# Turning key sums in one product group, a shorter warm-up and chunked weight multiplication in an attention and FFN kernel

## The chip, the cores and the metric

The kernel runs on one core of one Trainium2 chip. The metric is the device time of one execution in microseconds (us). A median of several executions is given for each kernel; some seven in ten executions lie within 0.3 us of it, single ones up to 1 us away. A ratio between two kernels is the mean time of one kernel's fast runs over that of the other's of the same rounds, so it is not quite the ratio of the medians. A profile is one execution; its span starts at the first instruction and is some 1.7 us shorter than the device time.

The engines are TensorE (PE in the profile; PEld is its weight load), VectorE (DVE), ScalarE (ACT), GpSimd (POOL) and SyncE (SP), which issues the loads.

## The reference

A polynomial sketch attention (4 batches, 4 heads, 1088 positions, head size 32) feeds a SwiGLU block of 128 to 1536 to 128:

```python
def phi(x):
    a = np.einsum('rd,bhsd->bhsr', S1, x)
    b = np.einsum('rd,bhsd->bhsr', S2, x)
    return np.einsum('bhsi,bhsj->bhsij', a, b).reshape(*x.shape[:-1], r * r)   # r = 8
q_p, k_p = (phi(q), phi(k))
kv = np.einsum('bhsf,bhsd->bhfd', k_p, v)
z = np.sum(k_p, axis=2)
num = np.einsum('bhsf,bhfd->bhsd', q_p, kv)
den = np.einsum('bhsf,bhf->bhs', q_p, z)[..., None] + 1e-06
x = (num / den)          # to (4352, 128)
g = x @ w_gate
out = (g * (1 / (1 + np.exp(-g))) * (x @ w_val)) @ w_out
```

The inputs come as 64-bit floats. The kernel narrows the weights itself: VectorE and ScalarE split exponent and mantissa, GpSimd multiplies the two parts.

## The kernel before

Batch 0 is computed first, with nothing beside it but the narrowing of weights; batches 1 to 3 are computed in pieces among the FFN products of the batch before. For each batch `key_values` sums k_p times v over the positions, and z, the sum of k_p, is added and turned so that the features stand on the partitions. Two steps did this for z: a group that adds (the result has 32 rows per head), and a turning by the identity, the same as for kv. In batches 1 to 3:

```python
        zs = feature_sums(phk)            # GpSimd: partial sums of k_p, 128 x 256
        ...
        key_values(kvp[:, 0, :], phk, 0, NC)
        for h in range(H):
            nc.tensor.matmul(
                kvp[32 * h : 32 * h + 32, 1, 0:F], ones[:], zs[:, h, :], start=True, stop=True
            )
        kvs = apool.tile([P, 2, F], FP32, tag="kvs", name="kvs")
        nc.scalar.copy(kvs[:], kvp[:, :, 0:F])
        ...
        for t in range(2):
            turn_kv(kvs[:, t, :], kzp[:, t, :])      # products with the identity, 2 halves each
        nc.scalar.copy(kvz[:], kzp)
```

Batch 0 does the same with `sel` in place of `ones`, and with VectorE copying between the steps (`zs0`, then `kvs0`). Its last third of `key_values` comes behind the adding group. Ahead of everything stand products of constants that nobody reads (`keep_warm`), which keep TensorE busy until the inputs arrive. The sketch (S1 and S2 turned into `s12`) comes behind them; then VectorE transposes k:

```python
    keep_warm(98, 32)
    keep_warm(18, 64)
    ...
    for h in range(H):                    # the sketch
        nc.tensor.matmul(srep[32 * h : 32 * h + 32, 0 : 2 * R], s32[:], ident[...], ...)
    keep_warm(3, ps=bank("acc"))          # 3 products of 512 columns
    ...                                   # s12 on VectorE
    for c in fpieces:
        turn_k(*c)
```

The loads are issued in the order S1, k, part of q, weight pieces 0 of gate and value, v (four parts), the rest.

Of the kernel before, what the change touches and what calls it, by code (L numbers as in the profile page):

```python
# [7 lines left out]
FP32 = mybir.dt.float32  # L8
# [4 lines left out]
ALU = mybir.AluOpType  # L13
# [4 lines left out]
def kernel(  # L18
# [28 lines left out]
    nc = tc.nc  # L47
    P = nc.NUM_PARTITIONS
    B, H, S, Dh = q.shape
# [6 lines left out]
    F = R * R  # L56
# [18 lines left out]
    apool = ctx.enter_context(tc.tile_pool(name="attn", bufs=1))  # L75
# [7 lines left out]
    def bank(tag=None):  # L83
        if tag is None:
            tag = free_banks[turn[0] % len(free_banks)]
            turn[0] += 1
        return psum.tile([P, TB], FP32, tag=tag, name="bank")

    def wide(tag):
        return psum.tile([P, 2, TB], FP32, tag=tag, name=tag)  # L90
# [8 lines left out]
    wg = const.tile([P, NCH, P], FP32, name="wg")  # L99
# [30 lines left out]
    weights = dict(wg=(wg, moe_w_gate), wv=(wv, moe_w_val), wo=(wo, moe_w_out))  # L130
# [36 lines left out]
    ident = const.tile([P, P], FP32, name="ident")  # L167
    ones = const.tile([P, Dh], FP32, name="ones")
    own = const.tile([P, H], FP32, name="own")
    sel = const.tile([P, Dh], FP32, name="sel")  # L170
# [17 lines left out]
    def keep_warm(n, w=TB, ps=None):  # L188


        if ps is None:
            ps = bank(free_banks[turn[0] % len(free_banks)])
        for _ in range(n):
            nc.tensor.matmul(  # L194
                ps[0:32, 0:w], warm[:, 0:32], warm[:, 0:w], start=True, stop=True
            )

    def narrow(dst, raw, shape):






        words = raw.bitcast(I32)
        pat = "p (n w) -> p n w" if len(shape) == 2 else "p c (n w) -> p c n w"
        words = words.rearrange(pat, w=2)
        lo = words[..., 0].bitcast(U32)
        hi = words[..., 1]
        first = len(shape) == 2  # L210
        tag = "s" if first else ""
        e, m = (
            stage.tile(shape, I32, tag=n + tag, name=n, bufs=6) for n in ("exp", "man")
        )
        f = m[:].bitcast(FP32)
        nc.vector.tensor_scalar(e[:], hi, 0x7FF00000, None, op0=ALU.bitwise_and)  # L216
        nc.vector.tensor_scalar(
            m[:], hi, 0xFFFFF, 0x100000, op0=ALU.bitwise_and, op1=ALU.bitwise_or
        )
        yield  # L220
        nc.scalar.activation(e[:], e[:], AF.Relu, bias=rebias[: shape[0], :], scale=8.0)  # L221
        nc.scalar.activation(f, m[:], AF.Copy, scale=2.0**-20)  # L222
        yield
        nc.vector.scalar_tensor_tensor(  # L224
            out=e[:], in0=hi, scalar=-(1 << 31), in1=e[:],
            op0=ALU.bitwise_and, op1=ALU.bitwise_or,
        )
        nc.vector.scalar_tensor_tensor(  # L228
            out=f, in0=lo, scalar=2.0**-52, in1=f, op0=ALU.mult, op1=ALU.add
        )  # L230
        mul = nc.vector if first else nc.gpsimd
        mul.tensor_tensor(out=dst, in0=f, in1=e[:].bitcast(FP32), op=ALU.mult)  # L232
        if not first:
            load_next()
        yield
# [26 lines left out]
    def turn_q(x0, n):  # L262
        nc.vector.transpose(
            out=qT[:, x0 : x0 + n, :, :].rearrange("p x a t -> p (x a) t"),
            in_=qld[:, 2 * x0 : 2 * x0 + 2 * n, :],
        )
# [54 lines left out]
                stop=(c + 4 >= NC),  # L321
            )

    def turn_kv(kvs, kzp):

        for half in range(2):
            nc.tensor.matmul(  # L327
                kzp[F * half : F * half + F, 0:P], kvs, ident[:], start=True, stop=True
            )

    def query_products(x0, n, tags):

# [108 lines left out]
    def feature_sums(phk):  # L441

        rows = phk[:].rearrange("p c h i j -> p c (h i j)")
        s = apool.tile([P, 4, H * F], FP32, tag="zs", name="zs")
        add = lambda o, a, b: nc.gpsimd.tensor_tensor(out=o, in0=a, in1=b, op=ALU.add)  # L445
        add(s[:], rows[:, 0:4, :], rows[:, 4:8, :])
        add(s[:, 0:2, :], s[:, 0:2, :], s[:, 2:4, :])
        add(s[:, 0, :], s[:, 0, :], s[:, 1, :])
        add(s[:, 0, :], s[:, 0, :], rows[:, 8, :])
        return s[:, 0, :].rearrange("p (h f) -> p h f", h=H)  # L450

    def attention(b):

        for c0, c1 in kpieces:
            turn_k(c0, c1)
            if c1 == NC and b + 1 < B:
                load_k(b + 1)
            yield
        phk = apool.tile([P, NC, H, R, R], FP32, tag="phk", name="phk")
        prods = [key_products(wide(t)[:, 0, :], *c) for t, c in zip("ab", kpieces)]  # L460
        key_features(phk, prods[0], *kpieces[0])
        yield
        key_features(phk, prods[1], *kpieces[1])
        zs = feature_sums(phk)
        yield
        kvp = wide("a")
        key_values(kvp[:, 0, :], phk, 0, NC)
        for h in range(H):
            nc.tensor.matmul(
                kvp[32 * h : 32 * h + 32, 1, 0:F], ones[:], zs[:, h, :], start=True, stop=True  # L470
            )
        kvs = apool.tile([P, 2, F], FP32, tag="kvs", name="kvs")
        nc.scalar.copy(kvs[:], kvp[:, :, 0:F])
        if b + 1 < B:
            load_v(b + 1, [nc.sync] * 4)
        turn_q(*steps[0])
        yield
        kvz = apool.tile([P, 2, P], FP32, tag="kvz", name="kvz", bufs=2)
        kzp = wide("b")[:, 0, 0 : 2 * P].rearrange("p (t n) -> p t n", t=2)
        for t in range(2):  # L480
            turn_kv(kvs[:, t, :], kzp[:, t, :])
        nc.scalar.copy(kvz[:], kzp)
        kvz = kvz[:, 0, :], kvz[:, 1, :]
        yield
        tags = "ab"
        for i, (x0, n) in enumerate(steps):
            phq = query_features(n, query_products(x0, n, tags))
            if i + 1 < len(steps):
                turn_q(*steps[i + 1])
            elif b + 1 < B:  # L490
                load_q(b + 1)
            yield
            divide(b, x0, n, totals(n, phq, kvz, side_by_side(tags[0])))
            tags = tags[::-1]
            yield
# [5 lines left out]
    acc = {}  # L501
# [4 lines left out]
    def unit(i, j, late=False):  # L506

        t0, n = blocks[i]
        g, u = bank(), bank()
        for o, w in ((g, wg), (u, wv)):  # L510
            nc.tensor.matmul(  # L511
                o[:, 0:n], w[:, j, :], xT[:, t0 : t0 + n], start=True, stop=True
            )
        sg = fpool.tile(
            [P, BW], FP32, tag="sgl" if late else "sg", name="sg", bufs=6 if late else 3
        )
        nc.scalar.activation(sg[:, 0:n], g[:, 0:n], AF.Silu)  # L517
        hj = fpool.tile([P, BW], FP32, tag="h", name="hj", bufs=27)
        hidden[i, j] = hj
        todo.append((i, j))  # L520
        if late:
            nc.scalar.copy(hj[:, 0:n], u[:, 0:n])
            lates.append((hj[:, 0:n], sg[:, 0:n]))
        else:
            nc.vector.tensor_tensor(  # L525
                out=hj[:, 0:n], in0=sg[:, 0:n], in1=u[:, 0:n], op=ALU.mult
            )
# [38 lines left out]


    keep_warm(98, 32)
    keep_warm(18, 64)
    fills = {(w, i): narrow_w(w, i) for w in weights for i in range(len(pieces[w]))}  # L570

    def part(name, i):

        next(fills[name, i], None)
# [6 lines left out]
    for h in range(H):  # L581
# [4 lines left out]
            start=True,  # L586
            stop=True,
        )
    keep_warm(3, ps=bank("acc"))
    sTv = srep[:, 0 : 2 * R].rearrange("p (t r) -> p t r", t=2)  # L590
    nc.vector.tensor_tensor(
        out=s12[:],
# [24 lines left out]
    part("wg", 0)  # L617
    part("wv", 0)
    zq = apool.tile([P, H * F], FP32, tag="zq", name="zq")
    kvs, zs = (apool.tile([P, F], FP32, name=x) for x in ("kvs0", "zs0"))  # L620
    kvz = [apool.tile([P, P], FP32, name=x) for x in ("kvz0", "kvz1")]
    qbs.append(query_copy(n, *pss[1]))
    nc.scalar.copy(zq[:], kz)
    part("wg", 0)
    key_values(kv, phk, *fpieces[0])
    key_values(kv, phk, *fpieces[1])
    phq = query_features(n, pss, qbs)
    zp = bank("g2")
    for h in range(H):
        nc.tensor.matmul(  # L630
            zp[32 * h : 32 * h + 32, 0:F], sel[:], zq[:, F * h : F * h + F],
            start=True, stop=True,
        )
    key_values(kv, phk, *fpieces[2])
    nc.vector.tensor_copy(zs[:], zp[:, 0:F])
    turn_q(*steps[1])
    for t, s, to, tag in ((1, zs, None, "g0"), (0, kvs, kv, "g1")):
        if to is not None:
            nc.vector.tensor_copy(s[:], to)
        ps = bank(tag)  # L640
        turn_kv(s[:], ps)
        nc.scalar.copy(kvz[t][:], ps[:, 0:P])
    part("wv", 0)
    part("wg", 0)
    nd = totals(n, phq, kvz, ([bank(t) for t in ("g2", "acc")], side_by_side("a")[0]))
# [19 lines left out]
    part("wg", 2)  # L665
    part("wv", 2)
    turn_q(*steps[2])
    unit(0, 2, late=True)
    part("wg", 2)
    unit(1, 0, late=True)  # L670
    pss = query_products(*steps[2], "ab")
    qbs = [query_copy(steps[2][1], *ps) for ps in pss]
# [98 lines left out]
```

## Time and profile before

| | before |
|---|---|
| device time, median | 323.42 us (323.35 to 323.60, 3 runs) |
| span of the profile | 321.5 us |
| TensorE busy | 312.6 us, 97% |
| first FFN product | 16.06 us |
| FFN product that waits for weight piece 1 | 19.69 us |

The timeline of TensorE in batch 0 (start and busy time in us, engine, line, operation, form, count):

```profile
10.36 0.88 PE L304 MATMUL b<-phk,vld 128*32 128x64 f32 x48
11.05 0.31 PE L630 MATMUL bank<-zq,sel 128*32 128x64 f32 x8
11.18 0.51 PE L304 MATMUL b<-phk,vld 128*32 128x64 f32 x24
```

L304 is the product with v, L630 the group that adds the key sums: it stands for only 0.13 us between two parts of L304. And GpSimd's multiplication of the second pieces (L232), in its timeline:

```profile
18.46 1.18 POOL L232 TENSOR_TENSOR wg<-man,exp 128x256 f32<-128x256 f32 x1 [2.54 <-DVE man L228]
19.60 0.75 POOL L232 TENSOR_TENSOR wv<-man,exp 128x256 f32<-128x256 f32 x1
```

The second is the same work as the first and took 0.43 us less.

### The profile page before, as it was taken

The numbers are of one execution on the slowest core, as the hardware profiler recorded it, in microseconds if no ns is written. First come the engines' busy times: TensorE is split into PE (matmuls) and PEld (weight loads), VectorE is DVE, ScalarE is ACT, GpSimd is POOL, SyncE is SP. The second block draws the span as 40 slices with busy tenths as digits, with TensorE's granted clock in tenths as the row PEclk, the third lists the DMA queues.
The fourth block names the chain that finished last, engine by engine and source line by source line (L and its number), as shares of the span: only waits on it lengthen the run. The fifth ranks groups of instructions, "written<-read, shape, count | busy, mean of one in ns | idle before, by whom it ended". The sixth has DMA issues, their size and how long they took to land.

```text
span 321.5 us, 5554 instructions
## 1 busy us (share of the span) xinstructions
PE 312.6 (97%) x2276; PEld 189.9 (59%) x2276; DVE 156.7 (49%) x330; ACT 99.0 (31%) x227; POOL 37.6 (12%) x53
## 2 busy tenths in 40 slices
PE   8889999999999999999999999999999999999994
PEld 6545555656556665555666656555667655556672
DVE  4887888653466522544643543354544332322331
ACT  3467555322121222322322322323222222222220
POOL 2322333173000140000000060000000000000000
PEclk9999999999999999999999999999999999999998
DMA  7543580204041201100210100000010100100101
GB/s 203 156 150 100 157 248 0 71 0 96 1 96 22 69 17 55 27 0 2 31 65 0 22 2 0 14 12 2 0 27 0 20 0 2 26 0 0 24 2 20
DMA packets 25017, 13.99 MB, mean 44 GB/s; under 512 B 18848, under 2 KB 23072, under 8 KB 24992
## 3 DMA queue, kind: packets, MB, share of 16 engines
q1 hardware_dynamic: 24304, 13.56, 16.5%
q8 instruction: 18, 0.29, 0.4%
q10 hardware_dynamic: 688, 0.08, 0.2%
q14 instruction: 7, 0.06, 0.1%
HBM read 11.41 MB, written 2.23 MB: 42 GB/s over the span
## 4 chain that ended last, share of the span: by engine, by line
PE 89%; DVE 5%; ACT 2%; issue 1%; DMA 1%; POOL 0%; DVEq 0%
PE bank L511 50%; PE bank L539 28%; PE a L348 2%; PE a L398 2%; PE b L348 1%; PE bank L194 1%; PE a L304 1%; ACT exp L221 1%; DVE exp L216 1%; DMA raw<-in_moe_w_out_dram 1%; PE b L398 1%; PE a L273 1%; PE b L327 1%; PE bank L316 1%; ACT man L222 0%
## 5 line engine op out<-in xcount | busy, mean ns | idle before, releaser
L525 DVE TENSOR_TENSOR hj<-sg,bank 128x384 f32<-128x384 f32 (+1 forms) x138 | 72.7, 529 | 122.6 <-PE bank L511 117.8
L517 ACT ACTIVATE sg<-bank 128x384 f32<-128x384 f32 (+1 forms) x144 | 67.8, 473 | 167.1 <-PE bank L511 165.5
L511 PE MATMUL bank<-xT,wg 128*128 128x384 f32 (+1 forms) x288 | 114.1, 478 | 2.3 <-POOL wg L232 1.1
L511 PE MATMUL bank<-xT,wv 128*128 128x384 f32 (+1 forms) x288 | 111.9, 470 | 0.3 <-DVE hj L525 0.3
L539 PE MATMUL bank<-hj,wo 128*128 128x384 f32 (+1 forms) x288 | 109.1, 471 | 0.1
L511 PEld LDWEIGHTS bank<-xT,wv 128*128 128x128 f32 x288 | 54.0, 190 | 35.2 <-DVE hj L525 3.6
L511 PEld LDWEIGHTS bank<-xT,wg 128*128 128x128 f32 x288 | 52.5, 190 | 36.8 <-issue 3.9
L539 PEld LDWEIGHTS bank<-hj,wo 128*128 128x128 f32 x288 | 54.0, 190 | 33.0 <-issue 2.4
L445 POOL TENSOR_TENSOR zs<-phk 128x1024 f32<-128x1024 f32 x3 | 7.1, 2352 | 107.1 <-PE bank L511 106.0
L376 DVE TENSOR_TENSOR phq<-a,qb 128x384 f32<-128x384 f32 (+1 forms) x11 | 5.8, 531 | 10.7 <-ACT qb L362 10.7
L362 ACT COPY qb<-a 128x384 f32<-128x384 f32 (+1 forms) x11 | 5.1, 462 | 15.0 <-PE b L348 8.6
L348 PE MATMUL b<-qT,sq 32*64 32x192 f32 (+1 forms) x176 | 9.2, 324 | 0.0
L348 PE MATMUL a<-qT,sq 32*64 32x192 f32 (+1 forms) x176 | 9.2, 324 | 0.0
L221 ACT ACTIVATE exp<-exp,rebias 128x384 int32<-128x384 int32 (+3 forms) x15 | 8.3, 550 | 2.8 <-DVE exp L216 2.0
L419 DVE STREAM_TRANSPOSE dT<-a 128x384 f32<-128x384 f32 (+1 forms) x8 | 4.4, 550 | 7.8 <-PE a L398 7.8
L362 ACT COPY qb<-b 128x384 f32<-128x384 f32 (+1 forms) x11 | 5.1, 464 | 9.7 <-PE b L348 6.4
L224 DVE SCALAR_TENSOR_TENSOR exp<-raw,exp 128x384 int32<-128x384 int32 (+2 forms) x14 | 7.4, 532 | 0.9 <-ACT exp L221 0.9
L348 PEld LDWEIGHTS a<-qT,sq 32*64 32x64 f32 x176 | 5.5, 131 | 3.9 <-issue 3.0
L376 DVE TENSOR_TENSOR phq<-b,qb 128x384 f32<-128x384 f32 (+1 forms) x11 | 5.8, 527 | 4.2 <-ACT qb L362 4.2
L555 DVE STREAM_TRANSPOSE o<-bank 128x384 f32<-128x384 f32 (+1 forms) x12 | 6.7, 561 | 2.2 <-PE bank L539 1.8
L232 POOL TENSOR_TENSOR wg<-man,exp 128x384 f32<-128x384 f32 (+2 forms) x5 | 4.6, 928 | 21.1 <-DVE man L228 21.1
L228 DVE SCALAR_TENSOR_TENSOR man<-raw,man 128x384 f32<-128x384 uint32 (+2 forms) x14 | 6.9, 493 | 0.0
(93 smaller groups left out, 164.4 us busy)
## 6 DMA issues: line engine op xcount, KB each, us to landing
kld<-in_k_dram SPq DMA_DIRECT2D x4, 544.0 KB, 4.7
vld<-in_v_dram SPq DMA_DIRECT2D x12, 144.0 KB, 4.0
qld<-in_q_dram SPq DMA_DIRECT2D x3, 544.0 KB, 3.8
raw<-in_moe_w_out_dram SPq DMA_DIRECT2D x4, 384.0 KB, 3.2
out_dram<-o SPq DMA_DIRECT2D x32, 48.0 KB, 1.8
raw<-in_moe_w_gate_dram SPq DMA_DIRECT2D x3, 384.0 KB, 3.2
raw<-in_moe_w_val_dram SPq DMA_DIRECT2D x3, 384.0 KB, 3.4
out_dram<-o SPq DMA_DIRECT2D x14, 40.0 KB, 1.7
```

What stands on the lines that cost most here:

```text
L221: nc.scalar.activation(e[:], e[:], AF.Relu, bias=rebias[: shape[0], :], scale=8.0)
L224: nc.vector.scalar_tensor_tensor(out=e[:], in0=hi, scalar=-(1 << 31), in1=e[:], op0=ALU.bitwise_and, op1=ALU.bitwise_or,)
L228: nc.vector.scalar_tensor_tensor(out=f, in0=lo, scalar=2.0**-52, in1=f, op0=ALU.mult, op1=ALU.add)
L348: nc.tensor.matmul(parts[g][F * half : F * half + F, t, 0:w], sq[r, t, :, :].rearrange("p i j -> p (i j)"), qT[r, x0 : x0 + n, half, :], s ...
L362: nc.scalar.copy(qb[:, :, 0:w], both[:, :, 1, 0:w])
L376: nc.vector.tensor_tensor(out=phq[:, 2 * pr : 2 * pr + 2, 0:w], in0=both[:, :, 0, 0:w], in1=qb[:, :, 0:w], op=ALU.mult,)
L398: nc.tensor.matmul(halves(nd[t])[half][32 * h : 32 * h + 32, 0:w], kvz[t][r, 32 * h : 32 * h + 32], phq[r, h, 0:w], start=True, stop=True,)
L445: add = lambda o, a, b: nc.gpsimd.tensor_tensor(out=o, in0=a, in1=b, op=ALU.add)
L511: nc.tensor.matmul(o[:, 0:n], w[:, j, :], xT[:, t0 : t0 + n], start=True, stop=True)
L517: nc.scalar.activation(sg[:, 0:n], g[:, 0:n], AF.Silu)
L525: nc.vector.tensor_tensor(out=hj[:, 0:n], in0=sg[:, 0:n], in1=u[:, 0:n], op=ALU.mult)
L539: nc.tensor.matmul(acc[i][:, 0:n], wo[:, j, :], hidden.pop((i, j))[:, 0:n], start=(j == 0), stop=(j == NCH - 1),)
```

## The change

The intent: one group both turns and adds the key sums, so that a copy and half of the turning fall away; fewer unread products, so that the sketch comes sooner; the second weight pieces multiplied by chunk of 128 columns, so that the first chunk can be used sooner; and one step of the third piece issued ahead of a unit. The core of the diff:

```diff
-        mul.tensor_tensor(out=dst, in0=f, in1=e[:].bitcast(FP32), op=ALU.mult)
+        p2 = e[:].bitcast(FP32)
+        cuts = [slice(0, 1), slice(1, 2)] if shape[1] == 2 else [slice(None)]
+        for c in cuts:
+            mul.tensor_tensor(out=dst[:, c], in0=f[:, c], in1=p2[:, c], op=ALU.mult)
...
+    def turn_sums(sums, weights, ps):
+        for h in range(H):
+            for half in range(2):
+                nc.tensor.matmul(
+                    ps[F * half : F * half + F, Dh * h : Dh * h + Dh],
+                    sums[:, F * h : F * h + F],
+                    weights,
+                    start=True, stop=True,
+                )
...     # batches 1 to 3
-        for h in range(H):
-            nc.tensor.matmul(
-                kvp[32 * h : 32 * h + 32, 1, 0:F], ones[:], zs[:, h, :], start=True, stop=True
-            )
-        kvs = apool.tile([P, 2, F], FP32, tag="kvs", name="kvs")
-        nc.scalar.copy(kvs[:], kvp[:, :, 0:F])
+        turn_sums(zs, ones[:], kvp[:, 1, :])
+        kvs = apool.tile([P, F], FP32, tag="kvs", name="kvs")
+        kvz = [apool.tile([P, P], FP32, tag="kvz%d" % t, name="kvz", bufs=2) for t in range(2)]
+        nc.scalar.copy(kvs[:], kvp[:, 0, 0:F])
+        nc.scalar.copy(kvz[1][:], kvp[:, 1, 0:P])
...
-    keep_warm(18, 64)
+    keep_warm(9, 64)
...
-    keep_warm(3, ps=bank("acc"))
+    keep_warm(2, ps=bank("acc"))
+    keep_warm(16, 32, ps=bank("acc"))
...     # batch 0
-    for h in range(H):
-        nc.tensor.matmul(
-            zp[32 * h : 32 * h + 32, 0:F], sel[:], zq[:, F * h : F * h + F], ...
-        )
+    ps = bank("g2")
+    turn_sums(zq, sel[:], ps)
+    nc.scalar.copy(kvz[1][:], ps[:, 0:P])
     key_values(kv, phk, *fpieces[2])
-    nc.vector.tensor_copy(zs[:], zp[:, 0:F])
     turn_q(*steps[1])
...
-    unit(0, 2, late=True)
     part("wg", 2)
+    unit(0, 2, late=True)
```

More of the change, by code (lines that the diff above doesn't have):

```diff
@@ L322, in unit_sums, with turn_kv @@
             )
-    def turn_kv(kvs, kzp):
+    def turn_kv(kvs, ps):
         for half in range(2):
             nc.tensor.matmul(
-                kzp[F * half : F * half + F, 0:P], kvs, ident[:], start=True, stop=True
+                ps[F * half : F * half + F, 0:P], kvs, ident[:], start=True, stop=True
             )
+    def turn_sums(sums, weights, ps):
[5 more added lines that the diff above has]
+                    weights,
+                    start=True,
+                    stop=True,
+                )
     def query_products(x0, n, tags):
@@ L449, in feature_sums @@
         add(s[:, 0, :], s[:, 0, :], rows[:, 8, :])
-        return s[:, 0, :].rearrange("p (h f) -> p h f", h=H)
+        return s[:, 0, :]
     def attention(b):
@@ L477, in attention @@
         yield
-        kvz = apool.tile([P, 2, P], FP32, tag="kvz", name="kvz", bufs=2)
-        kzp = wide("b")[:, 0, 0 : 2 * P].rearrange("p (t n) -> p t n", t=2)
-        for t in range(2):
-            turn_kv(kvs[:, t, :], kzp[:, t, :])
-        nc.scalar.copy(kvz[:], kzp)
-        kvz = kvz[:, 0, :], kvz[:, 1, :]
+        ps = wide("b")[:, 0, :]
+        turn_kv(kvs[:], ps)
+        nc.scalar.copy(kvz[0][:], ps[:, 0:P])
         yield
@@ L619 @@
     zq = apool.tile([P, H * F], FP32, tag="zq", name="zq")
-    kvs, zs = (apool.tile([P, F], FP32, name=x) for x in ("kvs0", "zs0"))
-    kvz = [apool.tile([P, P], FP32, name=x) for x in ("kvz0", "kvz1")]
+    kvs = apool.tile([P, F], FP32, tag="kvs", name="kvs")
+    kvz = [apool.tile([P, P], FP32, tag="kvz%d" % t, name="kvz", bufs=2) for t in range(2)]
     qbs.append(query_copy(n, *pss[1]))
@@ L627 @@
     phq = query_features(n, pss, qbs)
-    zp = bank("g2")
-    for h in range(H):
-        nc.tensor.matmul(
-            zp[32 * h : 32 * h + 32, 0:F], sel[:], zq[:, F * h : F * h + F],
-            start=True, stop=True,
-        )
+    ps = bank("g2")
+    turn_sums(zq, sel[:], ps)
+    nc.scalar.copy(kvz[1][:], ps[:, 0:P])
     key_values(kv, phk, *fpieces[2])
-    nc.vector.tensor_copy(zs[:], zp[:, 0:F])
     turn_q(*steps[1])
-    for t, s, to, tag in ((1, zs, None, "g0"), (0, kvs, kv, "g1")):
-        if to is not None:
-            nc.vector.tensor_copy(s[:], to)
-        ps = bank(tag)
-        turn_kv(s[:], ps)
-        nc.scalar.copy(kvz[t][:], ps[:, 0:P])
+    nc.vector.tensor_copy(kvs[:], kv)
+    ps = bank("g1")
+    turn_kv(kvs[:], ps)
+    nc.scalar.copy(kvz[0][:], ps[:, 0:P])
     part("wv", 0)
@@ L667 @@
     turn_q(*steps[2])
+    part("wg", 2)
     unit(0, 2, late=True)
-    part("wg", 2)
     unit(1, 0, late=True)
```

## The prediction

> **What bounds the kernel now.** I read the page's busy shares and chain first, then the chain of its first 20 us, then the timelines of the groups that the change touches. The page says that the span is TensorE work:
>
> ```profile
> PE 312.6 (97%) x2276; PEld 189.9 (59%) x2276; DVE 156.7 (49%) x330; ACT 99.0 (31%) x227; POOL 37.6 (12%) x53
> ...
> PE 89%; DVE 5%; ACT 2%; issue 1%; DMA 1%; POOL 0%; DVEq 0%
> ```
>
> Busy shares of a pipelined engine say little, so I checked the starts of the products: behind 20 us a 128x384 product starts every 0.323 us (two per matrix product), with extra gaps of more than 0.2 us only five times, all between 32 and 78 us. A product that is added or removed after about 80 us is therefore paid in full. Before 20 us another regime holds. The chain there (start, us, what) is:
>
> ```profile
> 4.90 0.34 PE bank L582 x8
> ...
> 5.33 0.23 DVE s L591
> 5.55 1.41 DVE kT L257 x3
> ...
> 12.14 0.12 DVE kvs L639
> ...
> 12.31 0.44 PE bank L327 x4
> ...
> 13.34 0.59 DVE dT L419
> ...
> 18.05 0.34 DVE man L228
> ...
> 18.46 1.19 POOL wg L232
> ...
> 19.69 4.20 PE bank L511 x12
> ```
>
> Here VectorE carries the work, and two hops hand over: the sketch (L582, S1 and S2 turned) before the key transposes, and GpSimd's multiplication of the second weight piece (L232) before the FFN unit. The view of waits gives that hop its price on TensorE:
>
> ```profile
> PE bank L511 <- POOL wg L232: 1.1, 1, 1.1
> ```
>
> From 19.69 us on TensorE runs almost without a gap to 28 us, and what follows hangs on it, so time won at 19.69 us should reach the end.
>
> For the product groups I used timelines of TensorE around 182, 194 and 200 us, in the steady part (batch 3; start, busy, line, form, count):
>
> ```profile
> 182.09 0.80 PE L273 MATMUL a<-s,kT 128*64 128x64 f32 x20
> 182.72 0.64 PE L273 MATMUL b<-s,kT 128*64 128x64 f32 x16
> 183.29 0.91 PE L511 MATMUL bank<-xT,wg 128*128 128x384 f32 x2
> ...
> 193.16 1.21 PE L304 MATMUL a<-phk,vld 128*32 128x64 f32 x72
> 194.19 0.29 PE L469 MATMUL a<-zs,ones 128*32 128x64 f32 x8
> 194.42 0.91 PE L511 MATMUL bank<-xT,wg 128*128 128x384 f32 x2
> ...
> 200.42 0.66 PE L327 MATMUL b<-ident,kvs 128*64 128x128 f32 x8
> 201.01 0.59 PE L511 MATMUL bank<-xT,wg 128*128 128x384 f32 x1
> ```
>
> The starts are what to read: 72 of L304 go in 1.03 us (14 ns each, four column groups side by side), 36 of L273 in 1.20 us (33 ns with the way out; 29 ns start to start, as two every 58.5 ns), the 8 of L469 cost 0.23 us and the 8 of L327 0.59 us (55 ns start to start, plus 0.20 us on the way out).
>
> **What the Trainium skill says.** "TensorEngine Tiling (Array Packing)", Overview, Key Properties: a change of tiling mode drains TensorE. The trace agrees: a 384-column product followed by one of another shape (128*32, 128*64, 64*32) takes 0.415 us to the next start, not 0.323, so 0.09 us per change. "TensorE: Matmul & The Clock Gate", LDWEIGHTS: a weight load costs its columns over 1.2 GHz, so 64 columns would be 53 ns, by the page. The trace gives 58.5 ns per pair of halves for L273 (64 weight columns, 64 moving) but 56 ns per four for L304 (32 weight columns, also 64 moving): I read the difference as the 64-column load being the limit in L273. "SBUF — State Buffer", Terms and "SBUF: two separate sides": VectorE instructions with two SBUF inputs and GpSimd exclude each other for whole instructions. The trace agrees: the same 128x256 multiplication on GpSimd took 1.18 us at 18.46 us, under two such VectorE instructions that end at 19.06 us, and 0.75 us at 19.60 us.
>
> **The change part by part.**
>
> *Turned sums.* Before, each batch added the key sums in 8 instructions (4 products of 64 columns, 32-column weights) and turned them in 4 of the 8 instructions of L327. After, 16 instructions (4 heads, 2 halves, two passes) have the sums as 64-column weights and only 32 moving columns. Streaming 32 columns would allow about 14 ns each (half of 27 ns, two halves at once), but the weight load should hold them at L273's pitch of 29 ns. In batches 1 to 3: before 0.23 + 0.59 = 0.82 us. After: mode change behind L304 0.09 us, 16 x 29 ns = 0.46 us, way out 0.12 us, together 0.67 us; L327 with 4 instructions fewer is 0.59 - 4 x 0.055 = 0.37 us; sum 1.04 us. That is +0.22 us per batch and, all three lying in the steady part, +0.67 us. ScalarE's copies become three (about 0.19, 0.27 and 0.27 us) in place of 0.27 and 0.37 us; it is 31% busy, which costs nothing.
>
> *The same in batch 0.* VectorE loses a copy of 0.23 us (L635) and TensorE the first L327, but that copy is not what the end waits for: kvs comes at 12.07 us behind the transposition of q, while its products were done at 11.69 us. After the change the 16 products stand ahead of the last 24 of L304: instead of 0.13 us they take 0.09 + 0.46 + 0.12 = 0.67 us. The last L304 ends at about 12.25 us rather than 11.69, and kvs starts at about 12.30 rather than 12.07: +0.2 us on the chain.
>
> *Unread products.* Nine products of 64 columns at 53 ns are 0.48 us less before the sketch, which moves from 4.90 to about 4.4 us. But the transposes behind it need k: that load is issued at 1.26 us and lands 4.0 us later, at 5.28 us. They start at 5.47 us now and can start at 5.35 at best: -0.1 us. The 16 short products in place of one of 512 only keep the array busy for as long.
>
> *Multiplication by chunk.* The unit needs only the first 128 columns of the piece. A 128x128 multiplication took 0.46 us elsewhere; with the 0.43 us that it is shut out, the first half ends near 19.35 us rather than 19.65. wv follows at 19.35 + 2 x 0.42 = 20.2 us, so its product can start at about 20.24 us instead of 20.44. Gain about 0.25 us.
>
> *Order.* ScalarE converts the third piece before the third unit; ScalarE and VectorE both have idle time there (VectorE idles 0.95 us at 23.67), and TensorE does not wait on either between 20.5 and 28 us. 0.
>
> Sum: +0.67 + 0.2 - 0.1 - 0.25 = +0.5 us, so 323.9.
>
> **The rivals.** First: the weight load is not the limit, and the 16 products go at 14 ns. Then a batch costs 0.09 + 0.22 + 0.12 + 0.37 = 0.80 us, as before, and batch 0 loses nothing; -0.35 us in all, 323.1. For it speaks that the pitch of 29 ns rests on one group; against it, that L273 and L304 differ only in the weight columns and the column groups that follow from them. I give it 0.3. Second: k does not gate (or lands earlier) and the full 0.48 us of the shorter warm-up comes through: 0.35 us better than the sum. Against it stands the landing time. Third: the shorter warm-up lets the array get its full clock later; the first products ran at half pace (53 ns for 64 bf16 columns at 4 us, 220 ns for 512 at 5.5 us), so a later switch could cost up to 1 us. Against it: the stretch up to the transposes is filled as before. Fourth: a piece multiplied earlier starts the next weight loads earlier and upsets the DMA order; the loads are released by VectorE's reading of the raw piece, not by GpSimd, so I expect nothing.
>
> **Range and chances.** 0.7 x 323.9 + 0.3 x 323.1 is about 323.7. The repeats of before lie within 0.25 us. The lower end takes the first and second rivals together, 322.7; the upper end takes a slower pitch (40 ns: 16 x 11 ns x 3 = 0.5 us more) or a little of the third, 324.5. Two per cent is 6.5 us, and no part is larger than 1 us: within 2% is all but certain.
>
> **What would show it.** The new group's starts per instruction: 29 ns (sum right) or 14 (first rival), and the time from the last L304 product of batch 3 to the next FFN product: 0.7 us against 0.26. The first transposition of k at 5.35 us. kvs in batch 0 at 12.2 (12.3 less 0.1). First use of the second wg piece at 19.5 us. From there to 170 us the distance between the same FFN products of the two traces should grow by 0.22 us at each batch; if it grows elsewhere, or if the full clock comes later, the prediction is wrong.

## The result

The changed kernel took 324.70 us (median of 4 runs, 324.49 to 324.88) against 323.51 (323.35 to 323.78, 4 runs): ratio 1.0036, 95% interval 1.0018 to 1.0053. It is slower by 1.2 us, which is within 2%, and it lies 0.2 us above the upper end of the range on record. The direction was right, the size was not.

The page's busy shares and the chain by engine:

```profile
PE 313.4 (97%) x2298; PEld 190.6 (59%) x2298; DVE 156.6 (48%) x329; ACT 98.9 (31%) x230; POOL 37.8 (12%) x55
...
PE 88%; DVE 5%; DMA 2%; ACT 2%; issue 1%; POOL 0%; SPq 0%; DVEq 0%
```

TensorE has 0.8 us more busy time, and the chain now contains a load (DMA 2%, was 1%). The chain of the first 20 us says which:

```profile
1.26 4.19 DMA kld<-in_k_dram
...
5.47 1.50 DVE kT L260 x3
...
10.97 0.88 PE b L307 x48
11.85 0.59 PE bank L338 x16
12.44 0.52 PE b L307 x24
...
12.98 0.24 DVE kvs L645
...
14.29 0.59 DVE dT L434
...
19.42 0.91 POOL wg L235
...
20.37 4.32 PE bank L522 x12
```

The transposes of k start at 5.47 us, as in before, though the sketch is done 0.48 us earlier: they wait for k. L307 (the product with v, L304 before) starts at 10.97 in place of 10.36 us, and L338, the new group, takes 0.59 us between the two parts of L307 where the old one took 0.13. The view of waits names both loads:

```profile
PEld b L307 <- DMA vld<-in_v_dram: 0.8, 1, 0.8
...
DVE kT L260 <- DMA kld<-in_k_dram: 0.5, 1, 0.5
```

The timeline of TensorE in batch 3, against the same stretch in the prediction:

```profile
194.47 1.21 PE L307 MATMUL a<-phk,vld 128*32 128x64 f32 x72
195.61 0.66 PE L338 MATMUL a<-ones,zs 128*64 128x32 f32 x16
196.20 0.91 PE L522 MATMUL bank<-xT,wg 128*128 128x384 f32 x2
...
202.20 0.44 PE L330 MATMUL b<-ident,kvs 128*64 128x128 f32 x4
202.57 0.91 PE L522 MATMUL bank<-xT,wg 128*128 128x384 f32 x2
```

From L307's start to the next FFN product it is 1.73 us, was 1.26; the turning of kv is 0.37 us, was 0.59. GpSimd's timeline for the second pieces (the line is now L235):

```profile
19.42 1.31 POOL L235 TENSOR_TENSOR wg<-man,exp 128x128 f32<-128x128 f32 x2 [2.55 <-DVE man L228]
20.70 0.86 POOL L235 TENSOR_TENSOR wv<-man,exp 128x128 f32<-128x128 f32 x2
```

**Where the time came from.** Both kernels have the same 864 FFN product instructions in the same order, so I took the distance between the starts of the same one in the two traces, and list where it changes:

| start in before, us | distance, us | step | what lies there |
|---|---|---|---|
| 16.06 | +0.953 | +0.953 | batch 0 |
| 19.69 | +0.679 | -0.274 | first chunk of wg |
| 20.44 to 20.83 | +0.794 | +0.115 | wv, second chunks |
| 74.79 | +1.264 | +0.470 | batch 1, turned sums |
| 79.34 | +1.045 | -0.219 | batch 1, turning of kv |
| 118.97 | +1.522 | +0.477 | batch 2, turned sums |
| 125.56 | +1.304 | -0.218 | batch 2, turning of kv |
| 194.42 | +1.780 | +0.476 | batch 3, turned sums |
| 201.01 | +1.562 | -0.219 | batch 3, turning of kv |

Everywhere else it stays constant within 0.03 us. Batches 1 to 3 thus cost 0.251 + 0.259 + 0.257 = 0.77 us, and the chunks gave 0.16 us. The first row, 0.953 us, needs the experiments: part of it is v's late landing in this one execution. The full clock came early in this profile (its record begins at 4.27 us), so a late clock has no part in it.

### The profile page after: what moved, and what is told of

Its sections match the earlier page's. It is cut to its first block, busy times and chain, and to the rows that moved or that the text cites. A ratio compares the mean times of both kernels' runs of the same rounds, so it can differ in the third digit from the quotient of the medians.

```text
span 323.0 us, 5603 instructions
## 1 busy us (share of the span) xinstructions
PE 313.4 (97%) x2298; PEld 190.6 (59%) x2298; DVE 156.6 (48%) x329; ACT 98.9 (31%) x230; POOL 37.8 (12%) x55
## 4 chain that ended last, share of the span: by engine, by line
PE 88%; DVE 5%; DMA 2%; ACT 2%; issue 1%; POOL 0%; SPq 0%; DVEq 0%
PE bank L522 50%; PE bank L550 28%; PE a L363 2%; PE a L413 2%; DMA kld<-in_k_dram 1%; PE b L363 1%; PE a L307 1%; ACT exp L221 1%; DVE exp L216 1%; DMA raw<-in_moe_w_out_dram 1%; PE b L413 1%; PE a L276 1%; PE a L338 1%; PE bank L319 1%; ACT man L222 0%
## 5 line engine op out<-in xcount | busy, mean ns | idle before, releaser
L235 POOL TENSOR_TENSOR wg<-man,exp 128x128 f32<-128x128 f32 (+1 forms) x6 | 4.8, 802 | 20.7 <-DVE man L228 20.7
```

## The experiments

Theory A: the product groups cost the time, in all four batches. Theory B: v's late landing is brought about by the change and is the main cost. Later I called V the theory that the loads gate the start-up and scatter from execution to execution, and W that the shorter warm-up lets TensorE's full clock come late in some executions. All runs gave correct results. "Start" in the tables is the distance from the profile of before at its FFN product of 16.06 us, and "rest" is how much the distance has changed by 201.01 us; both are read from one execution, as above. The profile of before that they are measured from is of a fast execution (323.16 us).

### One part at a time

**e1_steady**: before, with the turned sums in batches 1 to 3 alone (the change's diff above, that part; other tags).

```diff
-        for h in range(H):
-            nc.tensor.matmul(
-                kvp[32 * h : 32 * h + 32, 1, 0:F], ones[:], zs[:, h, :], start=True, stop=True
-            )
+        turn_sums(zs, ones[:], kvp[:, 1, :])
...
+        nc.scalar.copy(kvs[:], kvp[:, 0, 0:F])
+        nc.scalar.copy(kvz[1][:], kvp[:, 1, 0:P])
```

> Before plus one part: the turned sums in batches 1 to 3 alone (16 products of 32 moving columns in place of 8 + 4). Theory A (the product groups cost the time): each of the three batches adds 0.25 us of TensorE work that nothing hides, as the two traces show at 74.8, 119.0 and 194.4 us, so +0.75 us, about 324.2 us; the group should take about 0.59 us from its first product to the next group. Theory B (the late landing of v in batch 0 is what costs, and the groups only move work about): 0 to +0.3 us. The start up to 20 us should be as before in both.

**e2_batch0**: before, with the turned sums in batch 0 alone.

```diff
-            zp[32 * h : 32 * h + 32, 0:F], sel[:], zq[:, F * h : F * h + F],
...
+    turn_sums(zq, sel[:], ps)
+    nc.scalar.copy(kvz[1][:], ps[:, 0:P])
     key_values(kv, phk, *fpieces[2])
-    nc.vector.tensor_copy(zs[:], zp[:, 0:F])
```

> Before plus one part: the turned sums in batch 0 alone. Theory A: kvs starts 0.3 us later than in before when v lands as early as there, because 16 products with a mode change on each side stand ahead of the last 24 products with v; +0.3 us at the end, about 323.8 us. Theory B: v is not touched by this part, so the first product with v still starts at 10.4 us; if it starts near 10.9 us here too, then the shift of v is not due to the warm-up.

**e3_warm**: before, with the shorter warm-up alone.

```diff
-    keep_warm(18, 64)
+    keep_warm(9, 64)
...
-    keep_warm(3, ps=bank("acc"))
+    keep_warm(2, ps=bank("acc"))
+    keep_warm(16, 32, ps=bank("acc"))
```

> Before plus one part: the shorter warm-up (9 products fewer, 16 short ones in place of one long). Theory A: the sketch comes 0.48 us earlier, the first transposition of k waits for its load as before, and the time stays within 0.1 us of before. Theory B (the warm-up shifts the fetches or the loads so that v lands late): the first product with v starts near 10.9 us in place of 10.4, +0.3 to +0.6 us. The forecast on record had -0.1 us.

**e4_chunk**: before, with the chunks alone.

```diff
-        mul.tensor_tensor(out=dst, in0=f, in1=e[:].bitcast(FP32), op=ALU.mult)
+        cuts = [slice(0, 1), slice(1, 2)] if shape[1] == 2 else [slice(None)]
+        for c in cuts:
+            mul.tensor_tensor(out=dst[:, c], in0=f[:, c], in1=p2[:, c], op=ALU.mult)
```

> Before plus one part: the second weight pieces multiplied by chunk on GpSimd. The product that waits for them starts 0.25 to 0.3 us earlier (at 19.4 in place of 19.69 us), the gain is carried to the end less about 0.1 us that the second operand takes back: -0.15 to -0.25 us, about 323.2 us. A rival: the two GpSimd instructions more are shut out by VectorE once more each, and the gain is gone: 0.

| kernel | median (lowest to highest), us | ratio to before | start | rest |
|---|---|---|---|---|
| e1_steady | 324.75 (324.00 to 325.25) | 1.0039 | +0.99 | +0.76 |
| e2_batch0 | 323.65 (323.60 to 323.97) | 1.0008 | +0.45 | 0 |
| e3_warm | 323.55 (323.38 to 324.33) | 1.0007 | +0.50 | 0 |
| e4_chunk | 323.25 (322.94 to 323.60) | 0.9993 | +0.21 | -0.16 |
| before, same rounds | 323.42 (323.17 to 323.78) | | | |

The rest of e1_steady is theory A's number: 0.76 us, at the three expected places. But its start is 0.99 us late, although it does nothing new in batch 0: there the last part of v landed at 11.29 us. In e3_warm and e4_chunk it was 10.79 and 10.52, in before 10.26, in e2_batch0 10.15. From the first product with v to the copy of kvs it is 1.68 us in each of e1, e3 and e4, and 1.71 in before. So v's landing carried the start-up of these three executions and of the changed kernel's, and it ranged from 10.15 to 11.29 us with no order by part: theory B falls as the main cost, theory V stands. In the changed kernel the same distance is 12.98 - 10.97 = 2.01 us: batch 0's group costs 2.01 - 1.68 = 0.33 us. e2_batch0 measured +0.08% (0.26 us), which agrees, though its interval (0.9995 to 1.0021) holds zero too. e4_chunk gives 0.16 us by its trace and 0.2 by the measured times, less than the 0.25 us of the prediction.

### The pitch of the group, and the loads

**e5_wide** tests why the group is slow: e1_steady with 64 moving columns.

```diff
-                    ps[F * half : F * half + F, Dh * h : Dh * h + Dh],
+                    ps[F * half : F * half + F, F * h : F * h + F],
...
-        turn_sums(zs, ones[:], kvp[:, 1, :])
+        turn_sums(zs, ones2[:], kvp[:, 1, :])      # ones2: 128 x 64
```

> As e1_steady, but each of the 16 products of a group has 64 moving columns in place of 32 (the same weights; half of the result isn't read). Theory L (the load of 64 weight columns sets the pitch): the starts stay at one pair of products every 58 ns and the group keeps its length of 0.59 us from its first product to the next group. Theory M (the moving columns or their way through set it): pairs slower than 58 ns, by up to 27 ns, and the group is up to 0.2 us longer.

Its timeline of TensorE in batch 3:

```profile
195.12 0.69 PE L337 MATMUL a<-ones,zs 128*64 128x64 f32 x16
195.74 0.91 PE L524 MATMUL bank<-xT,wg 128*128 128x384 f32 x2
```

The group takes 0.62 us with twice the moving columns, 0.59 with 32. In both, pairs of products follow each other every 58 to 59 ns; the 0.03 us are one longer first gap. The moving columns are not the limit here. That leaves the loading of 64 weight columns (theory L), which the next run tests. This is one execution, but these starts repeat to 1 ns from group to group.

**e6_quarters** uses that: before, with turned sums of 32 weight columns per product, four column groups, in all four batches. The edit is shown against the changed kernel's turning function.

```diff
-            for half in range(2):
+            for part4 in range(4):
+                f0 = F * h + 32 * (part4 % 2)
                 nc.tensor.matmul(
-                    ps[F * half : F * half + F, Dh * h : Dh * h + Dh],
-                    sums[:, F * h : F * h + F],
+                    ps[32 * part4 : 32 * part4 + 32, Dh * h : Dh * h + Dh],
+                    sums[:, f0 : f0 + 32],
```

> Before with the turned sums in all four batches, but in quarters: 32 weight columns per product, four column groups side by side, 32 products of 32 moving columns. Theory L: four products go in about 30 ns (a load of 32 columns takes half as long), the group takes 8 x 30 ns = 0.24 us plus 0.15 us, and there is no change of tiling mode behind the products with v; with four products less in the turning of kv (-0.22 us) each steady batch is 0.09 us shorter than in before, and kvs in batch 0 starts no later than in before: -0.2 to -0.6 us in all, about 323.0 us. Theory M (the number of products sets it, not the weight columns): 32 products at 29 ns are 0.93 us, and each batch is 0.7 us longer than before, about 326 us.

Its timeline of TensorE in batch 3:

```profile
194.43 0.48 PE L336 MATMUL a<-ones,zs 128*32 128x32 f32 x32
194.84 0.91 PE L520 MATMUL bank<-xT,wg 128*128 128x384 f32 x2
```

Twice as many products take 0.41 us, against 0.59 for the halves, and there is no change of tiling mode behind L304 (128*32 on both sides). Four products, one per column group, follow each other every 28 to 32 ns in the first six rounds. With L304 (32 weight and 64 moving columns: four every 56 ns) and the pairs above (64 weight columns: 58 ns with 32 or 64 moving ones) all four cases are measured: the time of a round followed the larger of the two column counts. Each steady batch is 0.04 us shorter than in before, where 0.09 was expected. 323.36 us (323.16 to 323.64), ratio 0.9997: the same as before within the scatter. The profile also shows something else: the products with k started at 6.52 us although k's first transpose started at 5.47, as in before, where they started at 6.09. The unread 512-column products ahead of them followed each other at 0.40 to 0.43 us in place of 0.22 to 0.33. The trace's record of the granted clock begins at 6.45 us here and at 5.38 us in before.

**e7_vfirst** and **e8_after_vfirst** take v out of the way: before and the changed kernel with v's load issued ahead of the first weight pieces.

```diff
+    load_v(0, [nc.sync] * 4)
     for i in range(NRAW if wide_w else len(coming)):
         if i == 2:
-            load_v(0, [nc.sync] * 4)
             load_q(0, 2 * XS, 4 * XS)
```

> Before with the load of v issued ahead of the first two weight pieces. Theory V (the landing of v, between 10.2 and 11.3 us in the profiles so far, gates the first product with v and makes the start-up scatter): the first product with v no longer waits for a load, starts at 10.2 to 10.4 us in every profile, and the times scatter less; the median is at or up to 0.3 us below before, unless the weight pieces now land too late for VectorE at 9.2 us, which would cost up to 0.5 us. Theory A alone (v is not on the path): same as before.

> The changed kernel with the same reordering of the loads. Theory A + V: with v out of the way the difference to e7_vfirst is that of the product groups and the chunks: 3 x 0.25 + 0.3 to 0.45 - 0.2 = +0.85 to +1.0 us. If v had been late because of the change itself (theory B), the difference would fall well below that, to 0.5 us or less, and this kernel would be much faster than the changed one (324.7).

e7_vfirst took 322.98 us (322.91 to 323.44), ratio 0.9989 (interval 0.9977 to 1.0001): 0.35 us below before, and the first product with v started at 9.83 us without a wait for its load. It supports theory V, at the edge of what five rounds resolve; in its profile the gain of 0.17 us comes from k (transposes at 5.30 in place of 5.47 us), not from v. e8_after_vfirst took 324.32 us (323.96 to 325.07), ratio 1.0027. The difference of the two ratios, 0.38% or 1.2 us, is more than theory A's 0.85 to 1.0 and far from theory B's 0.5. Its six executions fall apart: 323.96, 324.02, 324.07, 324.57 and then 325.01 and 325.07, the last of them profiled. In that profile the record of the granted clock begins at 9.49 us, and the 36 products with k took 2.19 us in place of the 1.58 us of before.

### The rest: warm-up or scatter

**e9_longwarm**: the changed kernel with the warm-up of before.

```diff
-    keep_warm(9, 64)
+    keep_warm(18, 64)
...
-    keep_warm(2, ps=bank("acc"))
-    keep_warm(16, 32, ps=bank("acc"))
+    keep_warm(3, ps=bank("acc"))
```

> The changed kernel with the warm-up of before (9 products of 64 columns more, and three of 512). Theory A: the warm-up is worth nothing either way, because k lands at 5.1 to 5.7 us and gates the transpositions: 324.4 to 324.8 us, as the changed kernel. Theory W (the shorter warm-up leaves the array at half clock[...] in some executions, as in the profile of e8_after_vfirst, where the full clock came at 9.49 us): this kernel loses the slow executions, its median falls by 0.2 to 0.3 us, to about 324.4 us, and no execution is over 324.9.

**e10_no_sums**: the changed kernel without the turned sums (before, with the shorter warm-up, the chunks and the order).

Against before, it holds the diffs of e3_warm and e4_chunk and

```diff
-    unit(0, 2, late=True)
     part("wg", 2)
+    unit(0, 2, late=True)
```

> The changed kernel without the turned sums: before with the shorter warm-up, the chunks and the new order. Theory A (the product groups are the whole loss): 323.2 us, as before less the 0.2 us of the chunks. If other parts lose too (the warm-up by late clock in some executions), single executions at 324 us and a median of 323.4 us. In the profile the distance to before grows nowhere after 25 us.

**e11_steady_vfirst**: e1_steady with v first.

Its diff against before is those of e1_steady and e7_vfirst together.

> e1_steady with the load of v issued ahead of the first weights, to be compared with e7_vfirst (322.98). e1_steady measured +1.26 us where its groups account for 0.74 us. Theory A: the rest was scatter of the landing of k and v and of the clock; here the time is e7_vfirst + 0.74 = 323.7 us. If the rest belongs to the change of batches 1 to 3, about 324.2 us again.

**e12_best**: quarters in all batches, v first, chunks, order, and the warm-up of before.

Against the changed kernel, it holds the diffs of e6_quarters (its turning function), e7_vfirst and e9_longwarm together.

> What the runs point to: turned sums in quarters in all batches, v loaded first, the second pieces by chunk, the new order, the warm-up of before. Sum of the parts: e7_vfirst 322.98, quarters 3 x -0.04 in the steady batches and about -0.1 in batch 0, chunks -0.2: about 322.6 us, below both kernels. A rival: the start-up is held by the loads and the clock whatever the products do, and it stays at 323.0 us.

| kernel | median (lowest to highest), us | ratio to before | start | rest |
|---|---|---|---|---|
| e9_longwarm | 324.30 (324.03 to 324.67) | 1.0023 | +0.55 | +0.59 |
| e10_no_sums | 323.17 (322.88 to 323.95) | 0.9989 | +0.23 | -0.17 |
| e11_steady_vfirst | 324.17 (323.93 to 324.39) | 1.0019 | +0.21 | +0.77 |
| e12_best | 322.92 (322.64 to 322.96) | 0.9977 | -0.17 | -0.28 |
| before, same rounds | 323.51 (323.22 to 324.13) | | | |

Without the turned sums the loss is gone (e10_no_sums), with one execution of five at 323.95. e11_steady_vfirst missed its 323.7: 324.17. Its rest is the 0.77 us again; its start is 0.38 us later than that of e7_vfirst, because k came later (transposes at 5.68 against 5.30 us). Even so, by the ratios e1_steady is 0.5 us slower than before plus its groups, and e11_steady_vfirst 0.2 us slower than e7_vfirst plus its groups. Both have the long warm-up. I can name only the scatter of the loads for it, which is not shown. e12_best beats both kernels: 322.92 us, 0.9977 of before (interval 0.9965 to 0.9990) and 1.8 us below the changed kernel. It scatters the least, too.

The parts read from traces sum to 0.77 + 0.33 - 0.16 = +0.94 us. e9_longwarm has them and measured +0.23%, 0.74 us; the changed kernel measured +1.2. The last four runs, on one chip, ask whether the warm-up makes that difference. They are e13_after_again (the changed kernel), e14_longwarm_again, e15_warm_again and e16_before_again, each the kernel named, unchanged.

> The changed kernel once more, on one chip with the next three. The parts read from the traces sum to +0.94 us (0.77 steady batches, 0.33 batch 0, -0.16 chunks), 324.4 us; it measured +1.19. Theory S (scatter of the landing of k and v and of the clock): 324.3 to 324.7 us, and no difference to e14_longwarm_again beyond 0.15 us. Theory W (the shorter warm-up lets the clock come late in some executions): 0.3 to 0.4 us above e14_longwarm_again, with single executions up to 1 us above the lowest.

> The changed kernel with the warm-up of before, once more. Both theories: 324.3 us (before + 0.94). Theory W: at least 0.3 us below e13_after_again; theory S: within 0.15 us of it.

> Before with the shorter warm-up, once more. Theory W: 0.3 us above e16_before_again, one execution in three or so near 324.3 us. Theory S: within 0.15 us of it.

> The kernel before itself, as a null: what difference five rounds show where there is none. Both theories: within 0.15 us of the runs of before in the same call; if it comes out 0.3 us away, differences of that size in the other runs mean nothing.

| kernel | median (lowest to highest), us | ratio to before | start | rest |
|---|---|---|---|---|
| e13_after_again | 325.05 (324.19 to 325.36) | 1.0046 | +0.42 | +0.61 |
| e14_longwarm_again | 324.48 (324.07 to 324.93) | 1.0033 | +0.38 | +0.61 |
| e15_warm_again | 323.74 (323.23 to 324.38) | 1.0009 | +0.82 | -0.02 |
| e16_before_again | 323.46 (323.24 to 324.46) | 1.0006 | +0.45 | -0.01 |
| before, same rounds | 323.40 (323.10 to 324.17) | | | |

In the null, e16, equal code differs by 0.06 us in the median and by 0.2 us in the ratio, its profile starts 0.45 us later than that of before, and a lone execution 1 us up happens to before as well. So the start of one profile measures no change of that size. The changed kernel lies 0.13% (0.42 us) above its long-warm version. Over all executions it is 324.82 us on average (10) against 324.41 (11), a difference of 0.41 us with a standard error of 0.14; part of these runs are of different calls. For e15 alone the difference is not resolved: e3 and e15 together average 323.71 (11), e16 and the runs of before in its call 323.50 (17), 0.21 with an error of 0.15. A third comparison shows none: e10_no_sums is e4_chunk with the shorter warm-up and the order, and it is not slower (0.9989 against 0.9993). The profile of e15_warm_again caught a late clock once more; the record begins at 9.29 us. Its products with k, in the timeline:

```profile
6.26 2.19 PE L273 MATMUL bank<-s,kT 128*64 128x64 f32 x36
```

and in the profile of before:

```profile
6.09 1.58 PE L273 MATMUL bank<-s,kT 128*64 128x64 f32 x36
```

The same 36 products take 0.61 us longer at the lower clock.

The kept profiles allow a finer check. In the 14 that have neither a late clock nor quarters, kvs of batch 0 starts, to within 0.02 us, at the later of two times: 6.60 us after the first transpose of k, or 1.78 us after the last part of v has landed. With the turned sums in batch 0 the two distances are 6.90 and 2.10 us. v decides in 9 of the 14, k in 5. In the two late profiles kvs comes 0.70 us (e8) and 0.78 us (e15) after that time. At 2 of 6 profiles this is, as an estimate, 0.25 us on average.

A late clock (over 9 us) appears in 2 of the 6 profiles with the shorter warm-up and in none of the 12 with the long one, where the record begins at 4.04 to 6.45 us. If the warm-up made no difference, both late ones would fall among these 6 of 18 by chance in 15 of 153 cases, about one in ten. So theory W is supported but not shown: 6 profiles are few, e10_no_sums speaks against it, and no slow execution of e13 was profiled (its profile is of the fastest one, 324.19 us).

## Why the prediction was wrong

Two steps failed. The first is the sum of the costs: +0.5 us, +0.94 us in the traces. The ways in and out of the new group were mis-sized in all four batches, the chunks gave less, and the gain of the shorter warm-up came to nothing; the mechanism of the largest term was right. The second is the setting aside of the third rival, a later full clock: it did come in 2 of 6 profiles. What lies between +0.94 and the measured +1.2 us is not in any term of the sum, and its cause stays open.

**Turned sums in batches 1 to 3**: predicted +0.67 us, measured +0.77 (e1_steady and e11_steady_vfirst 0.76 and 0.77). The 64-column weight load does set the pitch, as e5_wide and e6_quarters show together. The 16 products go in pairs every 58 ns, as L273 does. What the sum left out is that the way in is 0.150 us from the last product with v (0.036 us in before), where I charged only 0.09 for the mode change, and that the way out is 0.153 us where I put 0.12. The first rival, a pitch of 14 ns, is refuted; giving it 0.3 took 0.2 us off the answer.

**Batch 0**: predicted +0.2 us, measured +0.33 (start of v's products to kvs: 2.01 us against 1.68), or +0.30 where k decides (6.90 against 6.60), and 0.04 more from kvs to the first FFN product (4.03 us against 3.99). The reason is the same, the mis-sized ways in and out. I also took the wait of kvs behind VectorE's transposition in before as slack, and it was spent as predicted.

**Unread products**: predicted -0.1 us; this gain did not come. That k gates was right: the transposes start at 5.473 us after and at 5.472 before, and over all profiles they start at 5.26 to 5.75, as k lands. So the sketch's 0.48 us earned nothing. What the shorter warm-up cost is not settled: 0.41 us (error 0.14) in the changed kernel, 0.21 (0.15) in before, none from e4_chunk to e10_no_sums. I named the mechanism as the third rival (a later full clock) and set it aside because "the stretch up to the transposes is filled as before". The late clock of e8 and e15 shows that this was no ground. Why it was late there is not shown: the pause ahead of the sketch, 0.34 us from start to start, is in both warm-ups. I also counted 220 ns for 512 columns as half pace; that is the full one, and the half is the 0.40 to 0.43 us seen in e6_quarters.

**Multiplication by chunk**: predicted -0.25 us, measured -0.16. The first chunk came 0.27 us earlier, near the 0.3 us worked out. But the second operand took back 0.115 us: wv's first chunk is done behind two chunks of wg, and the product with wv starts 0.82 us behind that with wg, where it was 0.75. I charged 0.05 for this.

**Order**: predicted 0; nothing in the traces moves there.

The traced parts sum to 0.77 + 0.33 - 0.16 = +0.94 us; with the estimate of 0.25 us for the late clock it is +1.2, against +1.2 measured first and +1.5 last (1.0046). This agreement proves little: e1_steady, with the long warm-up, lay 0.5 us above its parts as well. The profile's own +1.56 us is 0.94 for the parts and 0.62 for v, which landed at 10.89 us in that execution and at 10.26 in the one of before. I had not looked at v's landing at all: in the profile of before it came just ahead of its first product, so it looked like no wait. That is chance, and no part of the change: it moves between 10.06 and 11.29 us over the profiles of kernels that leave its load in place.

## What to carry to other kernels

When TensorE is the bound, replacing two small product groups by one saves nothing by itself: count the weight columns loaded, the moving columns and the changes of tiling mode, because with few moving columns the weight load sets the pitch, and narrower weights in more column groups can be faster than half as many wide ones. A warm-up is worth its length only up to what gates the next step, here a load, but cutting it gained nothing here, and two of six profiles with the shorter one had a late clock, which cost 0.7 to 0.8 us each. Before putting a start-up difference down to a change, look at when the loads landed in each profile: here two profiles of equal code differed by 0.45 us at the first FFN product, and e1_steady, which changes nothing before it, by 1 us.

## What the Trainium skill lacked or had wrong

- "TensorE: Matmul & The Clock Gate", Part 1, says that the full clock follows sustained activity in a free-running window of about 3.4 us. The runs fit that length but do not show it, since each trace holds one start of the full clock: 3.49 to 6.45 us in sixteen profiles, 9.29 and 9.49 us in the two late ones, and the late ones less 3.4 us fall at 5.9 and 6.1. The page doesn't say how much idle time a window may hold. Here an idle gap of some 0.3 us ahead of the sketch was there in both warm-ups, and the late clock showed only with the shorter one. Where the limit lies is left open.
- The same page, LDWEIGHTS, gives columns over 1.2 GHz, 53 ns for 64 columns. Pairs of products with 64 fp32 weight columns came every 58 to 59 ns, with 32 or with 64 moving columns. Rounds of four products with 32 weight and 32 moving columns came every 28 to 32 ns.
- The same page, Part 1, states that starts never come closer than about 25 ns, without naming tiles there; its Part 3 gives about 4 ns between different tiles. Products in four different column groups started 6 to 7 ns apart here within a round, and 32 of them took 0.41 us, 13 ns each with the way out.
- "TensorEngine Tiling (Array Packing)", Tiling Modes, Key Properties (the prediction calls it "Overview"), says that a mode change drains TensorE, without a figure: 0.09 us each behind a 384-column product (0.415 us to the next start in place of 0.323), and back in the full array the second product starts 0.427 us behind the first, 0.10 us more than usual.
- "SBUF — State Buffer", "SBUF: two separate sides", says that a VectorE instruction with two SBUF inputs and a GpSimd one that reads SBUF exclude each other for the whole instruction. Nothing here contradicts it; halving the GpSimd instruction did not get the first half past the wait (0.91 us, where the same size took 0.46 at 13.69 us; 1.31 us for the two chunks, 1.18 in one).
- "DMA: Bandwidth & Descriptors" gives no figure for how far apart in time the 16 engines end one load. The sixteenth part of v's last load landed 0.65 to 1.8 us behind the fifteenth, where the load was left in its place. An instruction fetch of 16 KB that took 0.96 to 1.25 us began between 5.1 and 5.6 us in those profiles; that it is what delays one engine is my guess and was not tested.
